# Decay of batch 1 by rank-one matmuls, f by one queue and its chain in two column pieces, under a new instruction order

## The chip, the cores and the metric

The kernel runs on one core of a Trainium2 chip. The metric is the device time of one execution in microseconds (us); less is better. The core has five engines, each with its own instruction queue worked in order: PE (TensorE, matmuls), DVE (VectorE), ACT (ScalarE), POOL (GpSimd) and SP (SyncE, which here only issues DMAs). Engines wait for each other by semaphores alone. Matmuls write to PSUM; ACT and DVE read it.

## The reference

Attention with a forget gate, then a bilinear feed-forward layer. Batch 8, 8 heads, 576 positions, head size 64; 4608 tokens, model width 512, inner width 1536.

```python
def _attn_ref(q, k, v, f):
    scores = scale * np.matmul(q, k.transpose(0, 1, 3, 2))
    log_f = np.log(np.clip(f, 0.0001, 1.0))
    cum = np.cumsum(log_f, axis=-1)
    decay = cum[:, :, :, None] - cum[:, :, None, :]
    scores = np.where(causal, -1000000000.0, scores + decay)
    scores = scores - np.max(scores, axis=-1, keepdims=True)
    attn = np.exp(scores)
    attn = attn / (np.sum(attn, axis=-1, keepdims=True) + 1e-09)
    return np.matmul(attn, v)

def _moe_ref(x, w_a, w_b, w_out):
    a = x @ w_a
    b = x @ w_b
    return a * b @ w_out
```

In a softmax row the term cum of the query is a constant and falls out, so the kernel only adds −cum of the key, a row of 576 numbers for each of 64 heads.

## The kernel before

**Tiling.** Two heads of a batch make a head pair t (t = 4·batch + pair, 0 to 31). The 576 queries of a pair are five row blocks i = 0 to 4 (four of 128, the last of 64), and block i sees i+1 key blocks. Scores are made in four groups: group 0 holds rows 1 and 0, group 1 row 2, group 2 row 3, group 3 row 4. In batches 0 and 1 they come in three PE stages, (0), (1) and (2, 3); later in two. Each group takes one of two PSUM score slots (`sc`). Per row block then follow: the decay and the row maximum on DVE, the exponential with its sum on ACT (L531, L527), the reciprocal on DVE (L541), the normalization on POOL (L549), the transpose of P (batch 0 by PE and an eviction copy, the rest by a DMA transpose that SP issues, L563), P·V on PE (L591, L607) and its copy to xT. The feed-forward layer works on tiles of 256, 384 or 512 tokens: 12 pairs of matmul groups psa and psb (L861), ACT's copy of psa (L213), DVE's product (L872), and the output matmuls pso (L881).

**The decay row.** `f_rows` (L168 to L173) loads f into `cum_f`, 64 heads with two copies each on 128 partitions: one copy by two DMAs of ACT's queue, the other by two of POOL's. Then come, over all 576 columns: clip (DVE, L184), LN (ACT, L186), a running sum with the sign turned (DVE scan, L187), a 16-bit copy (L189) and the low part (L190), which leave `crow`: the sums as a 16-bit high and a 16-bit low row. `cum_store` (L195) also writes the sums to DRAM (`cum_d`).

**Three ways to add the decay.** Batch 0 (`DECP`) adds it on PE: `qk_group` multiplies a column of ones at the head's two rows (`pick`) with `crow` into the score slot, and DVE only takes a maximum over both heads (`do_max`, L474), with ACT's exponential reading PSUM. Batch 1 (`PSPREAD`, t = 4 to 7) has the row spread over 128 partitions by two matmuls a pair (`spread_mm`, L442), copied to the SBUF tile `spread` by ACT or DVE (`spread_ev`), its last 64 columns filled with zeros by POOL (L449; those come from PE in group 3); DVE then adds it head by head in one instruction that also takes the maximum (`do_decay`, L500) and writes a copy of the scores to SBUF tile `S`, from which ACT reads. Batches 2 to 7 load `spread` from `cum_d` (L453), mask it on POOL (L459, L466) and use `do_decay` too.

**Order.** Every step is an `Op` with an engine, a cost for a planner, and what it depends on. The order of all 2336 ops is written out as the list `ORDER`, by op number; `CHOICE` gives the engine of each op that has a choice (P, D, A). Each engine's queue is the part of that list which falls to it. Around the places that matter below, the queues read so. PE at the start: transposes of q and k, scores 0.(0), spread 4, keys' second half, scores 0.(1), spread 4, and so on, with the first feed-forward matmul after pair 0's P transposes. SP, late in batch 1: transpose of pair 6 (rows 2, then rows 3 and 4), load of batch 3's q, transposes of pair 7 (rows 0 and 1; rows 3 and 4), load of batch 3's k, spread of pair 10, transpose of pair 7 (row 2). PE there: four output matmul groups, scores 9.(0), P·V of pair 7's rows 0 and 1, two output groups. The store of the sums is SP's ninth op, behind the first key load of batch 1. POOL's queue begins with its two f loads and the constants, then the casts of q and k.

Of the kernel before, what the change touches and what calls it, by code (L numbers as in the profile page):

```python
# [25 lines left out]
def kernel(  # L26
# [150 lines left out]

    o_f = Op("ACT", 2.05, f_load, prio=-310, land=0.3)
# [5 lines left out]
    o1 = Op("DVE", 0.45, lambda _: nc.vector.tensor_scalar(out=cw["f"], in0=cw["f"], scalar1=1e-4,  # L184
                                                           scalar2=1.0, op0=MAX, op1=MIN), [o_f, o_f2], prio=-300)
    o2 = Op("ACT", 0.7, lambda _: nc.scalar.activation(out=cw["l"], in_=cw["f"], func=LN), [o1, o_w], prio=-300)  # L186
    o3 = Op("DVE", 1.35, lambda _: nc.vector.tensor_tensor_scan(  # L187
        out=cw["f"], data0=cw["1"], data1=cw["l"], initial=0.0, op0=MUL, op1=SUB), [o2, o0], prio=-300)
    o4 = Op("DVE", 0.45, lambda _: nc.vector.tensor_copy(out=cw["h"], in_=cw["f"]), [o3], prio=-300)  # L189
    o5 = Op("DVE", 0.75, lambda _: nc.vector.scalar_tensor_tensor(  # L190
        out=crow, in0=cw["h"], scalar=lowrow[:, 0:1], in1=cw["f"], op0=MUL, op1=ADD), [o4, o_c], prio=-300)
# [4 lines left out]

    o6 = Op("SP", 1.1, cum_store, [o3], prio=-300, land=0.4)
    o_e = Op("ACT", 1.4, warm_table(EXP), [o2], prio=-300)
    for u in s_users:
        u.extend([o_f2, o0, o1, o2, o3, o4, o5, o6])  # L200
# [79 lines left out]
    PSPREAD = {t for t in range(4, 8)}  # L280
    DECP = tuple(range(1))
# [356 lines left out]
    def attention(t, base):  # L638
# [12 lines left out]
        if not direct:  # L651
            if t in PSPREAD:
# [3 lines left out]
                for h in range(2):  # L656
                    bm = Op("PE", 512 * COLS, lambda _, h=h: spread_mm(t, h), [o5, bc0] + bcs, prio=prio(0) - 5, mode="full", name=f"bm{t}")
# [15 lines left out]
        for gs in ([(0,), (1,), (2, 3)] if b in EARLY else [(0, 1), (2, 3)]):  # L673
            deps = [kq_ops[(w, b, pr)] for w in "qk"] + [o_c] + ([o5] if direct else bcs)
# [285 lines left out]
    for n in cuts:  # L960
# [3 lines left out]
        0 1 3 4 19 13 25 31 2 37 20 5 21 6 14 22 7 23 15 26 12 16 260 8 24 11 17 9 54 32 27 18 261 57 28 63 33  # L964
        30 58 262 65 29 59 64 55 263 34 69-71 36 99 264 60 66 35 102 38 39 41 234 10 144 103 108 110 109 104 40
# [3 lines left out]
        56 175 138 220 75 139 81 221 176 183 184 207 87 76-78 241 228 82 229 88 83 242 101 243 118 163 80 79 164  # L969
# [8 lines left out]
        384 385 460 470 301 467 468 289 386 290 296 297 469 291 292 232 1676-1678 479 317 298 1679 374 410 411  # L978
# [4 lines left out]
        1702 1704 420 1703 432 433 428 427 429 1705-1707 421 1708 306 307 1709 399 417 439 440 435 434 1710-1713  # L983
        446 447 441 482 1714 1716 358 1718 1715 442 1719 1720 422 1717 443 489 448 1722-1724 1721 491 498 359
        492 1725 499 505 506 1726 1728 1730 356 1727 493 500 449 357 1729 501 502 436 394 395 400 424 444 431
        430 527 423 445 450 494 490 512 1731 507 508 1732 513 483 488 1733 517 509 484 402 403 655 451 453
        1734-1736 518 495 514 519 520 1739 529 454 1740 531 455 521 532 545 538 539 546 510 438 437 511 497
        503 504 496 522 523 533 1737 1741 1744 1746 408 650 566 452 530 1742 534 1745 540 541 1747 515 516 409
        406 1748 542 535 552 553 547 548 1749-1754 1756 1757 554 537 656 528 536 549 550 544 407 524 1755 557
        1758 1759 485 567 651 551 543 1760-1762 558 555 1763-1765 559 560 1766 1767 657 525 569 1743 608 662 676  # L990
        667 658 1768 659 1769 570 573 1770 1771 456 580 561 457 587 574 581 588 571 652 1772 458 562 556 563-565
        1738 575 653 654 1774 1776 1773 582 576 1777 583 459 1775 1778 572 1780 1779 590 1781 1782 584 577 594
        1783 1784 1786 589 1785 1788-1790 595 1787 596 663 579 568 591 1791 599 600 609 593 585 586 592 668 578
        602 1792-1794 664 1795 601 666 611 615 603 597 598 665 629 616 613 623 617 605 604 660 718 1796 661 677
        719 618 1797-1799 630 622 1800 612 619 1802 625 1803 632 624 631 606 607 674 672 1804 1805 614 636 637
        633 1806 1808 1807 1809 1810 638 1811 610 641 1812 626 1813-1815 642 635 621 634 628 675 620 627 643
# [4 lines left out]
        740 726 1850-1852 741 735 734 728 1853 742 724 746 747 846 760 856 850 761 720 751 752 847 802 848 748  # L1001
        1855-1857 851 717 716 1801 763 753 852 754 861 1854 854 743 729 749 736 1858 730 738 744 737 731 750 767
# [58 lines left out]
        2315 2314 2317 2316 2319 2318 2321 2320 2322 2323 2326 2324 2327 2325 2328 2331 2329 2332-2334 2330 2335  # L1061
# [49 lines left out]
```

## Time and profile before

| what | us |
|---|---|
| median of 3 runs | 418.45 (417.01 to 418.51) |
| the profiled execution | 415.86 |
| its span, first to last instruction | 414.1 |
| DVE decay with maximum, 128-row forms, L500 | 0.28 (128 columns), 0.42 (256), 0.55 (384), 0.68 (512) |
| the same, 64 rows by 576 | 0.75 |
| DVE maximum of both heads, L474 | 0.42, 0.69, 0.96, 1.21; last row 0.75 |
| spread copy from PSUM, 128x512 | 0.68 on DVE, 0.58 on ACT |
| DMA transposes, issue to landing | 3.6 to 8.6, median 4.3 |
| mean granted PE clock | 0.996 of full speed |

A view by stretch gives each engine's busy time between two moments of the span. The timeline lists instructions with start, duration, engine, line and form, and in brackets how long the engine had been idle and what ended that. "SPq" is a DMA issue in SP's queue. The chain of waits follows the last instruction back to what released it, again and again. Durations of matmuls include their latency; the distance from one to the next is their cost in a full PE.

### The profile page before, as it was taken

The page shows a single profiled execution, that of the slowest core. Times are in us where ns is not written, and L with a number is a line of the kernel's source. Part 1 is how long each engine was busy: PE and PEld are TensorE (multiplying, and loading weights), DVE is VectorE, ACT ScalarE, POOL GpSimd, SP SyncE. Part 2 cuts the span into 40 slices and gives each one's busy share as a digit, 9 for nine tenths or more (in the row PEclk, how much of TensorE's full clock was granted, in tenths as well). Part 3 has the DMA queues.
Part 4 walks back from the last instruction along what each step waited for, and adds up shares of the span by engine and source line. Part 5 has one row for each costly group of instructions (what it writes and reads, how often), then busy time and mean ns, then how long its engine had stood idle before and what let it go on. Part 6 is the DMA issues. An engine that isn't in the chain of part 4 may idle for free.

```text
span 414.1 us, 10945 instructions
## 1 busy us (share of the span) xinstructions
PE 391.0 (94%) x3860; PEld 212.0 (51%) x3860; DVE 301.3 (73%) x1002; ACT 276.9 (67%) x788; POOL 254.7 (62%) x442
## 2 busy tenths in 40 slices
PE   0688999998999999999999999999999999999996
PEld 0445785765755544444444544454444444444552
DVE  2889998996878958867987889678777885342240
ACT  2786899775867797766777687687787583231231
POOL 8699698766876867674886687676675745000000
PEclk9999999998999999999999999999999999999999
DMA  8899799999999999999979999999689727300202
GB/s 272 175 220 258 172 210 228 236 206 268 294 239 218 286 229 192 267 215 281 192 206 249 237 271 220 246 211 244 170 181 221 185 57 145 116 1 2 101 2 77
DMA packets 153528, 80.72 MB, mean 195 GB/s; under 512 B 130784, under 2 KB 133344, under 8 KB 153472
## 3 DMA queue, kind: packets, MB, share of 16 engines
q1 hardware_dynamic: 149536, 75.01, 77.1%
q0 software_dynamic: 3856, 4.87, 7.0%
q8 instruction: 30, 0.49, 0.5%
q14 instruction: 26, 0.21, 0.2%
q10 hardware_dynamic: 80, 0.15, 0.1%
HBM read 52.20 MB, written 9.58 MB: 149 GB/s over the span
## 4 chain that ended last, share of the span: by engine, by line
PE 82%; ACT 5%; DVE 4%; DMA 4%; POOL 2%; issue 1%; SPq 1%; POOLq 0%; DVEq 0%; ACTq 0%
PE psa L861 22%; PE pso L881 21%; PE psb L861 21%; PE sc L390 9%; PE pv L591 5%; ACT PA L531 2%; PE psT L258 2%; DMA wout<-in_k_dram 2%; DVE st L474 1%; DMA xT<-PA 1%; PE psP L569 1%; DVE S L500 1%; ACT PB L531 1%; PE sc L607 1%; SPq L563 1%
## 5 line engine op out<-in xcount | busy, mean ns | idle before, releaser
L500 DVE CUSTOM_DVE_ANT_0 S<-sc,spread 64x576 f32<-64x576 f32 (+4 forms) x232 | 125.3, 561 | 8.3 <-PE sc L390 3.5
L861 PE MATMUL psa<-xT,wa 128*128 128x512 f16 (+2 forms) x528 | 115.8, 342 | 0.9 <-DVE ht L872 0.5
L861 PE MATMUL psb<-xT,wb 128*128 128x512 f16 (+2 forms) x528 | 115.6, 342 | 0.3 <-ACT PTB L213 0.3
L549 POOL TENSOR_SCALAR PA<-PA,st 128x128 f16<-128x128 f16 (+2 forms) x192 | 90.1, 483 | 21.0 <-DVE st L541 13.9
L872 DVE TENSOR_TENSOR ht<-psb,a 128x512 f16<-128x512 f32 (+2 forms) x132 | 77.7, 590 | 34.8 <-PE psb L861 28.3
L213 ACT CAST a<-psa 128x512 f16<-128x512 f32 (+2 forms) x132 | 66.4, 504 | 53.4 <-PE psa L861 46.6
L881 PE MATMUL pso<-wout,ht 128*128 128x512 f16 x432 | 99.0, 382 | 0.4 <-DVE osb L217 0.4
L531 ACT ACTIVATE PA<-S,st 128x256 f16<-128x256 f32 (+2 forms) x168 | 84.2, 505 | 12.6 <-DVE st L500 12.5
L549 POOL TENSOR_SCALAR PB<-PB,st 128x512 f16<-128x512 f16 (+1 forms) x96 | 67.8, 715 | 28.1 <-DVE st L541 12.0
L861 PEld LDWEIGHTS <-wb 128*128 128x128 f16 x528 | 50.8, 98 | 40.8 <-issue 0.4
L861 PEld LDWEIGHTS <-wa 128*128 128x128 f16 x528 | 49.0, 98 | 41.3 <-issue 2.6
L881 PEld LDWEIGHTS <-ht 128*128 128x128 f16 x432 | 40.9, 98 | 47.7 <-issue 1.1
L531 ACT ACTIVATE PB<-S,st 128x512 f16<-128x512 f32 x56 | 40.2, 719 | 13.6 <-DVE st L500 12.4
L390 PE MATMUL sc<-kT,qT 64*128 64x128 f16 (+5 forms) x480 | 43.8, 278 | 3.9 <-ACT PA L531 2.2
L531 ACT ACTIVATION_READ_ACCUMULATOR PA<-S,st 128x1 f32 x168 | 32.3, 192 | 0.0
L390 PEld LDWEIGHTS <-qT 64*128 64x128 f16 (+1 forms) x480 | 17.3, 97 | 26.7 <-issue 20.8
L527 ACT ACTIVATE PB<-S,st 128x576 f16<-128x576 f32 x28 | 21.7, 776 | 12.3 <-issue 5.4
L541 DVE RECIPROCAL st<-st 128x2 f32<-128x2 f32 x128 | 18.7, 157 | 14.6 <-ACT PB L531 8.2
L217 DVE CAST xT<-pv 128x512 f16<-128x512 f32 (+1 forms) x40 | 23.0, 576 | 7.5 <-PE pv L591 7.4
L500 DVE CUSTOM_DVE_ANT_1 S<-sc,spread 128x256 f32<-128x256 f32 x48 | 19.8, 419 | 10.3 <-PE sc L607 8.2
L466 POOL TENSOR_SCALAR_AFFINE_SELECT spread<-spread 128x256 f32<-128x256 f32 x24 | 9.8, 408 | 28.0 <-DVE st L500 27.9
L459 POOL TENSOR_SCALAR_AFFINE_SELECT spread<-spread 128x768 f32<-128x768 f32 x24 | 20.9, 872 | 9.1 <-DMA spread<-cum_d 9.1
(85 smaller groups left out, 418.1 us busy)
## 6 DMA issues: line engine op xcount, KB each, us to landing
spread<-cum_d SPq DMA_DIRECT2D x24, 576.0 KB, 5.8
out_dram<-osb SPq DMA_DIRECT2D x36, 256.0 KB, 3.3
q<-in_q_dram SPq DMA_DIRECT2D x15, 576.0 KB, 5.9
k<-in_k_dram SPq DMA_DIRECT2D x15, 576.0 KB, 5.4
v<-in_v_dram SPq DMA_DIRECT2D x32, 256.0 KB, 4.5
wout<-in_moe_w_out_dram POOLq DMA_DIRECT2D x3, 512.0 KB, 6.6
v<-in_v_dram SPq DMA_DIRECT2D x8, 128.0 KB, 5.1
wa<-in_moe_w_a_dram POOLq DMA_DIRECT2D x2, 512.0 KB, 7.5
```

Source lines behind the costliest of these rows:

```text
L213: nc.scalar.copy(out=out_, in_=in_)
L217: VEC[e].tensor_copy(out=out_, in_=in_)
L390: nc.tensor.matmul(out=dst, lhsT=lhsT, rhs=rhs, start=start, stop=stop, skip_group_check=True)
L459: nc.gpsimd.affine_select(out=c[:, :, 0:SM].rearrange("p h (j k) -> p h j k", k=128), in_=c[:, :, SM:2 * SM].rearrange("p h (j k) -> p h j ...
L500: nc.vector.tensor_tensor_reduce(out=o, in0=x, in1=y, scale=-1.0, scalar=3e38, op0=ADD, op1=MIN, accum_out=m)
L527: nc.scalar.activation(out=p_blocks(t, 4), in_=T[("s" if direct else "z", t, 4)], func=EXP, bias=st[:, 8:9], scale=sign, accum_out=st[:, 1 ...
L531: nc.scalar.activation(out=p_blocks(t, i)[:, :, h, :], in_=(T[("s", t, i)][:, h, :] if direct else T[("z", t, i)][:, h * n:h * n + n]).rea ...
L549: VEC[e].tensor_scalar(out=p, in0=p, scalar1=st[:, c:c + 1], scalar2=1.0, op0=MUL, op1=MUL)
L591: nc.tensor.matmul(out=o[HP[h], 128 * i:128 * i + 128], lhsT=vt[:, j, pr + NP * h, :], rhs=pt[:, base_blk[i] + 2 * block_at(t, i, j) + h, ...
L861: nc.tensor.matmul(out=p[:, 0:n], lhsT=w16[:, db, 128 * fb:128 * fb + 128], rhs=xTflat[db][:, t0:t0 + n], start=(db == 0), stop=(db == 3))
L872: nc.vector.tensor_tensor(out=ht[:, 0:n], in0=T.pop(("psb", t0, fb))[:, 0:n], in1=T.pop(("a16", t0, fb))[:, 0:n], op=MUL)
L881: nc.tensor.matmul(out=o, lhsT=T[("ht", t0, fb)][:, 128 * tb:128 * tb + 128], rhs=wout16[:, fb, :], start=(fb == 0), stop=(fb == 11))
```

## The change

`DECP` becomes batches 0 and 1, `PSPREAD` is empty: pairs 4 to 7 get the ones-times-crow matmuls of batch 0, DVE's maximum in place of the decay instruction, and exponentials that read PSUM. Their spread matmuls, spread copies and POOL fills are gone; `spread` and `S` are first used by batch 2. All four f loads are issued by ACT, one after the other. Clip, LN, scan, 16-bit copy and low part run for columns 0 to 255 and then 256 to 575; the second scan starts from the last sum of the first. Score group 0 waits for the first piece alone, the others for both; the table load for EXP waits for both LNs.

There are 2300 ops now, in a newly found order, with 91 engine choices for 99. Near the start: both q casts of the first half on DVE, ahead of the clip; two weight loads on POOL ahead of a q cast; scores 1.(0) ahead of the second half of q; four of the P-transpose copies moved from ACT to DVE and four key and query copies the other way; one value cast moved from DVE to POOL. On SP the store of the sums stands behind the first q load of batch 2, and late in batch 1 the queue reads: spread 10, load of batch 3's k, transposes of pair 6 (rows 3 and 4) and pair 7 (rows 0 and 1), load of batch 3's q, transposes of pair 6 (row 2), pair 7 (rows 3 and 4; row 2). PE's order around pair 7's P·V is the same as before, and the tiles of the feed-forward layer too.

```diff
     def f_load(_):
-        f_rows(nc.scalar, 0)
-
-    def f_rows(eng, c):
-        if not cw:
-            f_tiles()
         rows = f.rearrange("b (h p) s -> h b p s", h=2)
         for half in range(2):
-            eng.dma_start(out=cw["f"][64 * half + 32 * c:64 * half + 32 * c + 32, :], in_=rows[half])
+            for c in range(2):
+                nc.scalar.dma_start(out=cw["f"][64 * half + 32 * c:64 * half + 32 * c + 32, :], in_=rows[half])
...
+    def scan(lo, hi):
+        nc.vector.tensor_tensor_scan(out=cw["f"][:, lo:hi], data0=cw["1"][:, lo:hi], data1=cw["l"][:, lo:hi],
+                                     initial=cw["f"][:, lo - 1:lo] if lo else 0.0, op0=MUL, op1=SUB)
...
-    o_f2 = Op("POOL", 1.3, lambda _: f_rows(nc.gpsimd, 1), prio=-310, land=0.3)
...
+    for lo, hi in ((0, 256), (256, S)):
+        n = hi - lo
+        o1 = Op("DVE", 0.06 + 0.00073 * n, lambda _, lo=lo, hi=hi: clip(lo, hi), [o_f], prio=-300, name="fclip")
+        o2 = Op("ACT", 0.2 + 0.00083 * n, lambda _, lo=lo, hi=hi: nc.scalar.activation(
+            out=cw["l"][:, lo:hi], in_=cw["f"][:, lo:hi], func=LN), [o1, o_w], prio=-300, name="fln")
+        o3 = Op("DVE", 0.02 + 0.00232 * n, lambda _, lo=lo, hi=hi: scan(lo, hi), [o2, o0] + ([o3] if lo else []),
+                prio=-300, name="fscan")
...
-    PSPREAD = {t for t in range(4, 8)}
-    DECP = tuple(range(1))
+    PSPREAD = set()
+    DECP = tuple(range(2))
...
-            deps = [kq_ops[(w, b, pr)] for w in "qk"] + [o_c] + ([o5] if direct else bcs)
+            deps = [kq_ops[(w, b, pr)] for w in "qk"] + [o_c] + (crow_ops[:1 if gs == (0,) else 2] if direct else bcs)
...
     CHOICE = """
-        DPAAPPADPPADAPDAPDPAAAADDDDADDADDDDDDDDAADAADDDDDAAAAAADAADAAAADAADAAAAAADAAADAAAAADDADAADAAAAAAAAA
+        DPAADDAAPPADAPDAPPPDDDDDADDDDDDDAADAADAADAADADAADAADAADAADAADDAAAAAAAAAAADAAAAAAAADADAAADAA
```

More of the change, by code (lines that the diff above doesn't have):

```diff
@@ L165, in f_load, with clip, low_part, cum_store @@
     def f_load(_):
-        f_rows(nc.scalar, 0)
-    def f_rows(eng, c):
-        if not cw:
-            f_tiles()
         rows = f.rearrange("b (h p) s -> h b p s", h=2)
         for half in range(2):
-            eng.dma_start(out=cw["f"][64 * half + 32 * c:64 * half + 32 * c + 32, :], in_=rows[half])
+            for c in range(2):
+                nc.scalar.dma_start(out=cw["f"][64 * half + 32 * c:64 * half + 32 * c + 32, :], in_=rows[half])
     def warm_table(func):
         return lambda _: nc.scalar.activation(out=warm, in_=warm, func=func)
-    o_f = Op("ACT", 2.05, f_load, prio=-310, land=0.3)
+    def clip(lo, hi):
+        x = cw["f"][:, lo:hi]
+        nc.vector.tensor_scalar(out=x, in0=x, scalar1=1e-4, scalar2=1.0, op0=MAX, op1=MIN)
+    def scan(lo, hi):
+        nc.vector.tensor_tensor_scan(out=cw["f"][:, lo:hi], data0=cw["1"][:, lo:hi], data1=cw["l"][:, lo:hi],
+                                     initial=cw["f"][:, lo - 1:lo] if lo else 0.0, op0=MUL, op1=SUB)
+    def low_part(lo, hi):
+        nc.vector.scalar_tensor_tensor(out=crow[:, lo:hi], in0=cw["h"][:, lo:hi], scalar=lowrow[:, 0:1],
+                                       in1=cw["f"][:, lo:hi], op0=MUL, op1=ADD)
+    def cum_store(_):
+        for half in range(2):
+            nc.sync.dma_start(out=cum_d[:, half * S:half * S + S], in_=cw["f"][64 * half:64 * half + 32, :])
+    f_tiles()
+    o_f = Op("ACT", 4.05, f_load, prio=-310, land=0.3)
     s_users = [take(o_f, "S") for _ in range(2)]
-    o_f2 = Op("POOL", 1.3, lambda _: f_rows(nc.gpsimd, 1), prio=-310, land=0.3)
     o_c = Op("POOL", 4.5, lambda _: constants(), prio=-300)
@@ L183 @@
     o_w = Op("ACT", 2.2, warm_table(LN), [o0], prio=-300)
[L184 to L191, printed above, removed]
-    def cum_store(_):
-        for half in range(2):
-            nc.sync.dma_start(out=cum_d[:, half * S:half * S + S], in_=cw["f"][64 * half:64 * half + 32, :])
+    crow_ops, lns = [], []
+    o3 = None
+    for lo, hi in ((0, 256), (256, S)):
[5 more added lines that the diff above has]
+                prio=-300, name="fscan")
+        o4 = Op("DVE", 0.06 + 0.0007 * n, lambda _, lo=lo, hi=hi: nc.vector.tensor_copy(
+            out=cw["h"][:, lo:hi], in_=cw["f"][:, lo:hi]), [o3], prio=-300, name="fhi")
+        o5 = Op("DVE", 0.06 + 0.0013 * n, lambda _, lo=lo, hi=hi: low_part(lo, hi), [o4, o_c], prio=-300, name="flo")
+        crow_ops.append(o5)
+        lns.append(o2)
+        for u in s_users:
+            u.extend([o0, o1, o2, o3, o4, o5])
     o6 = Op("SP", 1.1, cum_store, [o3], prio=-300, land=0.4)
-    o_e = Op("ACT", 1.4, warm_table(EXP), [o2], prio=-300)
+    o_e = Op("ACT", 1.4, warm_table(EXP), lns, prio=-300)
     for u in s_users:
-        u.extend([o_f2, o0, o1, o2, o3, o4, o5, o6])
+        u.append(o6)
     o_p = Op("POOL", 4.0, lambda _: paddings(), [o_c], prio=-100)
@@ L656, in attention @@
                 for h in range(2):
-                    bm = Op("PE", 512 * COLS, lambda _, h=h: spread_mm(t, h), [o5, bc0] + bcs, prio=prio(0) - 5, mode="full", name=f"bm{t}")
+                    bm = Op("PE", 512 * COLS, lambda _, h=h: spread_mm(t, h), crow_ops + [bc0] + bcs, prio=prio(0) - 5, mode="full", name=f"bm{t}")
                     su = take(bm, "ff")
@@ L984 @@
[L984 to L993, printed above, removed]
@@ new lines @@
+        602 1775 625 585 574 597 599 639 592 605 1778 1780 1779 1777 606 633 643 607 635 634 1781 647 648 655
+        654 608 609 603 1782 1784 1783 1785 644 649 1786 1788 1790 661 662 645 1787 657 650 651 656 663 1789
+        1791-1793 646 1794 598 584 610 591 604 653 1765 682 636 808 724 612 611 668 809 1796 664 1795 1797 1798
+        613 1760 813 669 642 683 637 1799-1802 1804 1803 670 658 673 665 666 1805 674 667 659 1806 1808 1807 675
+        1810 676 1811 1812 671 1809 677 1813 679 652 660 672 678 685 810 1814 1815 689 703 697 687 690 696 704
@@ new lines @@
+        691 1816 692 698 706 1817 699 811 812 688 814 815 686 710 711 705 816 712 820 821 684 725 680 681 766
+        700 715 717 716 718 817 1819-1821 1824 727 1825 1826 713 719 693 731 745 707 714 721 701 708 720 746
+        1822 738 733 747 748 729 732 739 694 695 709 702 1818 818 825 1829 1831 740 1827 1830 741 734 1833 1834
+        1832 728 730 723 722 749 752 822 1835 753 826 726 767 1836 823 1837 824 754 1839 757 758 1838 759 755
+        1840-1842 760 769 761 771 773 787 780 742 781 788 774 819 750 762 763 743 756 751 744 827 1843 1844
@@ new lines @@
+        828 829 775 1845 1847 783 782 776 1846 772 1849 1850 790 789 1851 770 784 777 735-737 794 1848 795 1852
+        768 791 834 1823 832 1828 786 833 779 835 793 876 765 764 830 1853 1855 1854 799 800 1856-1858 796 797
+        801 802 778 792 785 1859 837 1861 1863 841 843 848 1862 850 918 1860 855 803 804 842 1864 839 856 838
+        849 1865 1867 1866 1868 798 805 857 858 851 852 1869 1870 844 859 919 853 877 840 862 845 860 854
+        1871-1875 847 846 863 864 1876 836 861 1002 1003 831 867 1877-1879 865 868-870 1880 806 1007 807 874 879
@@ new lines @@
+        1397 1312 1334 1335 1310 1398 2053 1399 1329 2054 1330 2055-2057 1408 1308 1417 2059 2058 1339 1331 1317
+        1319 1333 1324 1326 1340 2060 1318 1336 1341-1343 1325 1332 2061 2062 1304 1305 2063 1351 2064 1355
+        1362 1363 2065 2067 1400 2069 1344 1345 1357 2066 1365 1352 1353 1337 1369 1338 1356 1358 2068 1370 1359
+        2071 2070 1372 2072-2074 1364 1371 2075 2076 1354 1409-1411 2077 1376 1377 1373 1366 1403 1350 1381 2079
+        1378 2078 1383 1379 1382 1375 1374 1384 2080 1414 1346 1347 2032 1458 2027 2081 2082 1419 2083 2086 1423
@@ new lines @@
+        1530 1536 2134 1535 2135 1549 1511 2136 1531 1550 1553 1560 1561 1537 1567 1525 1554 1551 1568 2137 2139
+        2138 1555 2140 2141 1562 1569 1556 2142 1563 2143 1552 2145 1557 2144 1574 1564 1532 1513 1527 2146 1570
+        2147 1575 2148 1576 2149-2151 1538 1520 1526 1512 1539 1559 1540 1541 2154 2155 1558 1548 1565 1566 1579
+        1577 1580 1571 1573 1578 1572 1581 2152 1582 1583 2156 2159 2160 2157 1585 1584 2161 1542 2164 1543
+        1586 1587 2153 2158 2162 2165 1588 2166 1589 2167 2168 2163 2169-2171 2173 2175 2172 2174 2176 2177 2179
@@ L1062 @@
+        2293 2296-2298 2294 2299
     """
     CHOICE = """
-        DPAAPPADPPADAPDAPDPAAAADDDDADDADDDDDDDDAADAADDDDDAAAAAADAADAAAADAADAAAAAADAAADAAAAADDADAADAAAAAAAAA
+        DPAADDAAPPADAPDAPPPDDDDDADDDDDDDAADAADAADADAADADAADAADAADAADDAAAAAAAAAAADAAAAAAAADADAAAADAA
     """
```

85 lines of the change are left out of this document (30 added, 55 removed), and 75 rows, old and new, of the table ORDER.

## The prediction

> **What bounds the kernel now.** I read the page's busy shares first, then the busy time by stretch of the span, then the timeline at the two places where TensorE stands still, then the chain of waits.
>
> ```profile
> span 414.1 us, 10945 instructions
> PE 391.0 (94%) x3860; PEld 212.0 (51%) x3860; DVE 301.3 (73%) x1002; ACT 276.9 (67%) x788; POOL 254.7 (62%) x442
> ```
>
> TensorE (PE) is the bound on average, with 23 us idle. The stretches (us of the span, the stretch's length, then each engine's busy time, clock, DMA share, GB/s) say where:
>
> ```profile
> 0.00:10.00 10.00, 0.84 (x18) 0.53 (x18) 1.79 (x4) 1.91 (x3) 8.12 (x35) 1.00 0.81 272
> 10.00:14.82 4.82, 2.12 (x35) 1.50 (x35) 3.98 (x5) 3.86 (x7) 4.68 (x9) 1.00 1.27 220
> 14.82:38.70 23.88, 20.24 (x262) 12.34 (x262) 21.12 (x47) 17.84 (x61) 19.41 (x38) 1.00 0.99 220
> 38.70:90.00 51.30, 50.38 (x733) 36.10 (x731) 48.14 (x176) 45.62 (x140) 40.99 (x64) 1.00 1.05 211
> 90.00:100.00 10.00, 8.15 (x47) 3.79 (x45) 6.11 (x26) 4.96 (x16) 6.58 (x12) 0.83 1.08 249
> 100.00:400.00 300.00, 299.04 (x2723) 152.99 (x2723) 217.79 (x743) 200.56 (x562) 174.91 (x289) 1.00 0.82 192
> ```
>
> Until 14.8 the inputs and the decay row are the bound; from there to 38.7 (first feed-forward matmul) VectorE (DVE, 21.1 of 23.9 us) and batch 0's softmax; from 38.7 on PE, full but for one hole in 90 to 100, where the clock falls as well. After 100 the hole is under 1 us in 300, so whatever is gained or lost before 100 reaches the end unshortened. The two places (start, duration, engine):
>
> ```profile
> 8.81 0.73 DVE L184 TENSOR_SCALAR cum_f<-cum_f 128x576 f32<-128x576 f32 x1 [7.24 <-DMA cum_f<-in_f_dram]
> 12.73 1.28 DVE L190 SCALAR_TENSOR_TENSOR crow<-cum_l,lowrow,cum_f 128x576 f16<-128x576 f16 x1
> 14.07 0.50 PE L390 MATMUL sc<-crow,pick 64*128 64x256 f16 x4 [0.68 <-DVE crow L190]
> 14.82 1.02 DVE L474 TENSOR_REDUCE st<-sc 128x2 f32<-128x512 f32 x2 [0.81 <-PE sc L390]
> ...
> 89.60 0.98 SPq L243 DMA_DIRECT2D q<-in_q_dram  x1
> ...
> 90.69 1.23 SPq L563 DMA_TRANSPOSE xT<-PA  x1
> ...
> 95.44 0.36 PE L591 MATMUL pv<-xT,nv 128*64 128x128 f16 x6 [1.85 <-DMA xT<-PA]
> ```
>
> The clip of f waits for f's load until 8.81; crow is ready at 14.01 and the first scores end with it, although the keys were there at 12.88. At the second place head pair 7's P·V waits for a transpose that was queued behind a q load.
>
> **The change, term by term.**
>
> *Head.* The four f loads go out on ACT's queue. The two there now took 2.02 us, so four take about 4.0 and end near 4.85; the last begins near 3.85, against 2.2 for POOL's last now. The f loads and the stores of the sums took 3.6 to 6.3 us to land, so f lands at 7.5 to 10.2; I take 8.8, as now, near the middle. ACT's table load moves from 2.87 to about 4.9 and ends near 6.2: hidden. POOL loses 1.35 us of issue, so the constants end at about 5.8 for 7.2. The q casts move to VectorE, which waited until 8.81 anyway, at some 0.8 us each (its k cast took 0.83), after q has landed (4.0 us after 0.81): done by 6.5, with k by 7.4, so keys and queries are ready before f. From f's landing: clip of 256 columns 0.33 (0.73·256/576), LN 0.30 (of 0.68), scan 0.60 (of 1.36), cast 0.20, low part 0.57, and 0.1 for each of four handovers: 2.4 us, crow's first piece at 11.2. The second piece needs scan 0.76, cast 0.26, low part 0.71: 12.95. VectorE then takes its first maximum at 13.0, which now starts at 14.82: **−1.8**. ACT is ready for it: key copies at 10 to 11.3, the EXP table (1.28 and 0.20), a q cast 0.63 and a key copy 0.65 end near 14.0, and the first exponential now starts at 15.94. Ends: f at 7.5 gives −3.1, f at 10.2 gives −0.4; a further us of slip in the casts, +0.6.
>
> [...]
>
> *14.8 to 38.7.* Six of the eight spread matmuls go (cold, 0.54 us from one to the next, 3.2 us), with five VectorE copies of 0.68 (3.4 us of 21.1) and ACT's one of 0.58. In the chain of waits these hold ACT 0.47, PE 0.54 and 0.54, VectorE 0.60 and 0.60: 2.75 us. The new order also hands copies between ACT and VectorE: four P-transpose copies (2.7 us) go to VectorE, four key and query copies (3.0) leave it, so that evens out, and the second value cast (0.69) goes to POOL, which loses three fills of 0.2. Ends 0 (other work fills the places) and −2.75; I take **−1.5**, since VectorE was 88% busy and most of its loss counts.
>
> *PE in batch 1, 46 to 86.* Each head pair gains ten crow matmuls, 64-row halves side by side. In the chain of waits the two-group stage costs 1.24 us with the decay (18 matmuls) and 0.81 without (14): +0.43. The first two groups have 384 columns each; 256 columns take 0.11 at full clock (four feed-forward matmuls of 256 in 0.44), so 0.16 each. 0.75 a pair, 3.0 for four; the last pair's two warm spread matmuls (0.32 and 0.22) go: **+2.5**. PE is full there, so all of it counts; ends +1.9 (some of it falls into the 0.9 us of holes) and +3.0.
>
> *VectorE and ACT in batch 1.* Per pair ten decays (2·(281+417+548+681)+2·753 ns = 5.36 us) become five maxima (417+690+958+1213+746 ns = 4.02): 5.3 us less over four, off the bound. It costs nothing and brings nothing by itself; it helps the next term. The exponentials read PSUM for SBUF at the same length (476 against 508 ns for 256). What is lost is the early release of the score slots, the first rival.
>
> *The hole at 93.6 to 95.4.* PE idles 1.85 us and then runs at half clock: eight output matmuls 2.64 for 1.80, two feed-forward groups 0.85 each for 0.44, so 0.84+0.41+0.41 = 1.66 more; 3.5 together. In the new SP order pair 7's first transpose stands ahead of that q load (0.98 us and gaps, 1.1), PE reaches the place 2.5 us later against the softmax, and VectorE there is lighter. Both together are more than 1.85. Ends −3.5 (gone, with the clock loss) and +2 (the hole doubles, since a later transpose, pair 6's second, now stands behind the q load). I take **−2.5**, near the end where it closes.
>
> [...]
>
> *Costed at nothing.* The store of the sums moves in SP's queue from behind the first key load of batch 1 to behind a q load of batch 2 (issued at 46.2 now), with only the spread of pair 8 waiting for it, wanted after 80: 30 us of cover; without it the 3.7 us store and a 5.8 us spread load are bare. Weight loads move ahead on POOL, to about 10 us for 19.06: two issues of 0.67 in front of a q cast; they crowd the value loads, which nothing reads before the first P·V at 30.2. The rest of the order after 100 has the same matmuls; ends −0.9 (its hole) and +3.5 (one new hole like that at 94).
>
> Sum: −1.8 −1.5 +2.5 −2.5 = −3.3. The profiled execution took 415.86 (span 414.1 and 1.8 around it) and would be 412.6; it lies 2.6 under the median 418.45 of the runs shown, so I forecast 418.45 − 3.3 = **415.1**.
>
> **Rivals.** *Score slots hold PE, slower.* A score slot of batch 1 is now freed by VectorE's last decay; then by ACT's last exponential: for the first group a maximum pair (1.1) and four exponentials (1.8), 2.9 us for 1.1. With two slots, PE's next scores wait, and all feed-forward matmuls behind them in order. Batch 0 has just this: PE waited 2.2 us for ACT's PA exponentials and 0.2 for its PB. Against it: some 11 us pass per pair in batch 1 and the slots need about (2.9+2.2+2.6+1.5)/2 = 4.6. Price: 2.4 again in a full PE, one clock loss of 1.7, the hole left as it is: −1.8 −0.8 +2.5 +2.4 +1.7 = +4.0, **422.4**. It decides once such waits exceed about 3 us. *The hole stays.* Transposes take 3.6 to 8.6 us to land whatever stands ahead: −0.8, **417.6**. *f late by one queue.* f at 10.2: −3.3+1.4 = −1.9, **416.5**. *The order is no better on the chip than on paper* (a new hole after 100, +3.5): 0.2, 418.6.
>
> **How the numbers follow.** Half a per cent is 2.1 us, about what this kernel's runs can tell from no change. Forecast 0.48, slots 0.26, hole stays 0.10, f late 0.08, new hole 0.08. Faster takes the forecast, less 0.04 where its terms come out small, and half of f late: 0.48. Slower takes the slots and half of the new hole: 0.30. Same: 0.22. The likeliest case alone lies in 412 to 417; for 8 in 10 I go down to 411 (head and stretch at their ends, −7) and up to 422 (the slots' case, whose upper half is left out).
>
> **What would show it.** Clip near 8.8 and the first maximum near 13.0; first feed-forward matmul near 35.4 instead of 38.7; no idle over 1 us and no clock under 1.00 in 85 to 100; PE waits on ACT's exponentials in batch 1 under 1 us in sum. It is wrong if PE sits idle before score matmuls between 45 and 90, if f lands past 10, or if a stretch after 100 shows a clock under 1.00.

## The result and the profile after

The changed kernel takes 423.89 us (median of 4 runs, 421.49 to 425.69), the kernel before 417.73 beside it (4 runs, 416.90 to 418.51): a ratio of 1.0137, with a 95% interval of 1.0103 to 1.0171. It is 1.4% slower, where 0.8% faster was forecast, and it lies above the range. The profiled execution took 425.69 with a span of 424.0. So the two profiles stand 9.8 us apart while the medians differ by 6.2: before's profile (415.86) lies 1.9 below its median, the one after 1.8 above. Differences between the two profiles are read with that in mind.

The page after, span and busy time, and the same stretches as before (length, busy time with instructions of PE, weight load, DVE, ACT and POOL, clock, DMA share, GB/s):

```profile
span 424.0 us, 10909 instructions
...
PE 392.0 (92%) x3892; PEld 214.2 (51%) x3892; DVE 295.6 (70%) x943; ACT 273.8 (65%) x785; POOL 251.3 (59%) x435
```

```profile
0.00:10.00 10.00, 1.69 (x36) 1.10 (x37) 2.01 (x5) 2.67 (x4) 5.48 (x30) 1.00 0.83 265
10.00:14.82 4.82, 2.00 (x40) 1.66 (x41) 3.73 (x7) 3.59 (x7) 4.28 (x9) 1.00 1.25 194
14.82:38.70 23.88, 14.93 (x217) 10.39 (x214) 18.09 (x41) 16.67 (x60) 18.59 (x34) 0.93 0.82 186
38.70:90.00 51.30, 48.61 (x724) 34.27 (x717) 41.09 (x99) 38.22 (x119) 37.45 (x57) 1.00 0.99 209
90.00:100.00 10.00, 9.79 (x94) 5.95 (x91) 7.77 (x31) 5.53 (x21) 7.01 (x14) 1.00 1.09 229
100.00:400.00 300.00, 294.73 (x2683) 150.03 (x2683) 216.53 (x752) 201.18 (x566) 178.52 (x297) 0.99 0.86 196
```

DVE is 7 us lighter from 38.7 to 90, as the change meant, and 90 to 100 is fuller. But PE, which was full from 38.7 on, now loses 2.7 us there, 5.3 in the 300 us after 100 (before: 1.0), and from 14.8 to 38.7 it is 5.3 us less busy (45 matmuls fewer, at a clock of 0.93). In that last stretch DVE, ACT and POOL are less busy as well.

The place at the start, and that of a new hole at 190, in the timeline (start, duration, engine, line, form; in brackets the idle time before and what ended it):

```profile
0.80 3.44 ACTq L169 DMA_DIRECT2D cum_f<-in_f_dram  x4
...
10.65 0.75 DVE L176 TENSOR_SCALAR cum_f<-cum_f 128x256 f32<-128x256 f32 x2 [3.69 <-DMA v<-in_v_dram]
11.20 0.78 ACT L201 ACTIVATE cum_l<-cum_f 128x256 f32<-128x256 f32 x2 [3.82 <-DVE cum_f L176]
...
11.88 1.16 ACT L228 COPY kT<-psT 128x576 f16<-128x576 f16 x2
...
12.55 0.50 PE L405 MATMUL sc<-kT,qT 64*128 64x256 f16 x4 [4.52 <-ACT kT L228]
...
13.19 1.33 DVE L179 TENSOR_TENSOR_SCAN cum_f<-cum_f,cum_l 128x320 f32<-128x320 f16 x1
...
15.31 1.23 DVE L183 SCALAR_TENSOR_TENSOR crow<-cum_l,lowrow,cum_f 128x320 f16<-128x320 f16 x1
...
16.46 1.94 DVE L489 TENSOR_REDUCE st<-sc 128x2 f32<-128x512 f32 x4
...
179.41 3.71 SPq L578 DMA_TRANSPOSE PTA<-PA  x1
183.16 0.58 SPq L258 DMA_DIRECT2D q<-in_q_dram  x1
183.84 3.41 SPq L578 DMA_TRANSPOSE PTB<-PB  x1
...
192.29 0.25 PE L606 MATMUL pv<-PTB,nv 128*64 128x128 f16 x2 [1.62 <-DMA PTB<-PB]
```

The clip starts at 10.65 (before 8.81). The releaser in its bracket is a v load that landed about then; what it needs is f. ACT's key copies stand behind both LNs in ACT's queue, so PE has no scores until 12.55. The second piece then holds DVE until 16.5, and only behind it comes the first maximum, at 16.46 (before 14.82), although its scores were complete at 14.05.

PE's waits (us in total, times, longest):

```profile
PE sc L405 <- ACT PA L546: 6.7, 5, 3.0
PE psT L273 <- DVE q L230: 5.2, 1, 5.2
PE sc L405 <- ACT kT L228: 4.5, 1, 4.5
PE pv L606 <- DMA PTB<-PB: 2.6, 3, 1.6
```

The first row is the wait for a score slot; it was 2.2 us before. All but 0.3 us of it falls into batch 0, ahead of the first feed-forward matmul. At 190.7 PE stands 1.62 us for the transpose that was issued at 183.84 and landed at 192.24, and then runs at half clock for 3.4 us. It also ran at half clock for 3.4 us at 32.1. The mean granted clock was 0.992 in two of the four runs (spans 423.8 and 424.0, the second being the profiled one) and 0.999 and 1.000 in the others (419.8 and 420.6); where the other run with 0.992 lost it is not on record.

**One common measure.** The table lists moments of the span at which a feed-forward matmul (psa, psb or pso) of a given number starts, and PE's idle time (gaps over 0.2 us, added up from each kernel's matmul records) in the parts between them. The labels are those of the experiments below.

| kernel | 1st | 193rd | 289th | last | idle: before 1st | to 193rd | to 289th | after | sum |
|---|---|---|---|---|---|---|---|---|---|
| before | 38.7 | 85.4 | 107.7 | 409.9 | 14.8 | 0.6 | 1.8 | 0.8 | 18.0 |
| after | 39.0 | 91.7 | 111.2 | 419.9 | 19.7 | 2.4 | 2.1 | 2.8 | 27.0 |
| b_1q | 40.7 | 87.3 | 108.7 | 413.5 | 17.9 | 0.6 | 2.4 | 2.9 | 23.8 |
| b_dec | 37.9 | 96.5 | 115.0 | 422.4 | 17.6 | 6.2 | 0 | 5.3 | 29.1 |
| a_2q1p | 36.2 | 89.3 | 110.5 | 417.5 | 18.1 | 2.8 | 2.4 | 3.3 | 26.6 |
| a_2q | 35.4 | 87.9 | 108.1 | 414.1 | 17.0 | 2.7 | 2.6 | 2.3 | 24.6 |
| a_2q_nocrow | 35.4 | 87.6 | 107.3 | 414.3 | 17.2 | 4.1 | 2.3 | 3.3 | 26.9 |

Each row is one execution. A second profile of a_2q has the same first two moments within 0.1 us, but the 289th 1.1 us and the last 0.9 us earlier; so differences of a microsecond between rows mean little.

The last matmuls of before and after are 10.0 us apart, and PE's idle times 9.0. But 4.9 of this idle time stands ahead of the first feed-forward matmul, which comes only 0.2 us later, as less work stands ahead of it. Behind that matmul lie 9.7 us. By the distances from one matmul to the next they are: PE idle +4.1, crow matmuls +3.0, spread matmuls −0.5, 14 transposes of P that stood ahead of it before +1.6, and about 1.5 in small differences.

### The profile page after: what moved, and what is told of

It is laid out like the page before. It is cut to its first block, busy times and chain, and to the rows that moved or that the text cites. A ratio compares the mean times of both kernels' runs of the same rounds, so it can differ in the third digit from the quotient of the medians.

```text
span 424.0 us, 10909 instructions
## 1 busy us (share of the span) xinstructions
PE 392.0 (92%) x3892; PEld 214.2 (51%) x3892; DVE 295.6 (70%) x943; ACT 273.8 (65%) x785; POOL 251.3 (59%) x435
## 5 line engine op out<-in xcount | busy, mean ns | idle before, releaser
L515 DVE CUSTOM_DVE_ANT_0 S<-sc,spread 64x576 f32<-64x576 f32 (+2 forms) x192 | 105.6, 567 | 7.5 <-POOL spread L481 3.6
L564 POOL TENSOR_SCALAR PA<-PA,st 128x256 f16<-128x256 f16 (+2 forms) x192 | 89.4, 478 | 25.2 <-DVE st L556 21.2
L546 ACT ACTIVATE PA<-S,st 128x256 f16<-128x256 f32 (+2 forms) x144 | 72.1, 503 | 14.4 <-DVE st L515 14.4
L405 PE MATMUL sc<-kT,qT 64*128 64x256 f16 (+5 forms) x480 | 44.7, 279 | 13.0 <-ACT PA L546 6.7
L546 ACT ACTIVATE PB<-S,st 128x512 f16<-128x512 f32 x48 | 34.4, 717 | 10.7 <-DVE st L515 10.4
L489 DVE TENSOR_REDUCE st<-sc 128x2 f32<-128x512 f32 (+4 forms) x40 | 31.4, 802 | 3.4 <-PE sc L405 2.6
L546 ACT ACTIVATION_READ_ACCUMULATOR PA<-S,st 128x1 f32 x144 | 27.4, 190 | 0.0
L232 DVE COPY osb<-pso 128x512 f32<-128x512 f32 x17 | 11.7, 689 | 21.7 <-PE pso L896 21.6
```

Of the source, the lines that this page charges most:

```text
L232: VEC[e].tensor_copy(out=out_, in_=in_)
L405: nc.tensor.matmul(out=dst, lhsT=lhsT, rhs=rhs, start=start, stop=stop, skip_group_check=True)
L489: nc.vector.tensor_reduce(out=m, in_=T[("s", t, i)], axis=AXX, op=MAX, negate=True)
L515: nc.vector.tensor_tensor_reduce(out=o, in0=x, in1=y, scale=-1.0, scalar=3e38, op0=ADD, op1=MIN, accum_out=m)
L546: nc.scalar.activation(out=p_blocks(t, i)[:, :, h, :], in_=(T[("s", t, i)][:, h, :] if direct else T[("z", t, i)][:, h * n:h * n + n]).rea ...
L564: VEC[e].tensor_scalar(out=p, in0=p, scalar1=st[:, c:c + 1], scalar2=1.0, op0=MUL, op1=MUL)
```

## The experiments

Labels with b_ are edits of the kernel before in its own order, with a_ of the changed kernel in the new order. Ratios are against the kernel before, run beside them.

### The change in its parts

**b_dec**: the decay of batch 1 alone, in the old order (without the spread instructions; seven score stages and one maximum stand a few places later, where a score slot is free).

```diff
-    PSPREAD = {t for t in range(4, 8)}
-    DECP = tuple(range(1))
+    PSPREAD = set()
+    DECP = tuple(range(2))
```

> The kernel before with the decay of batch 1 on PE alone: f by two queues, the chain in one piece and the order of before (score stages of pairs 3 to 8 a few places later, so that a score slot is free). Theory 'head, decay and holes each have a share': PE pays 2.5 us after 38.7, VectorE's relief gives 1.5 back before it, the hole at 94 closes in part: -1 to +2 us against before. Rival 'score slots': PE waits for ACT's exponentials between 45 and 90 for over 2 us, +4 us or more. Rival 'only the order and the f chain cost': the forecast holds without them, -2 us or better.

429.10 us, ratio 1.0275 (1.0232 to 1.0318). Its waits of PE, and what stands at the longest one:

```profile
PE sc L390 <- ACT PA L531: 9.1, 9, 2.7
```

```profile
45.92 1.61 DVE L474 TENSOR_REDUCE st<-sc 128x2 f32<-128x512 f32 x2
...
47.52 0.40 DVE L474 TENSOR_REDUCE st<-sc 128x2 f32<-128x256 f32 x1
...
47.96 0.47 ACT L531 ACTIVATE PA<-sc,st 128x256 f16<-128x256 f32 x1 [0.60 <-DVE st L474]
```

Scores made at 45.3 are read by the maximum, and only then by ACT's exponentials from 47.96; PE stands 2.68 us at 48.0 for that slot and then runs at half clock for 6.8 us. The first rival's mechanism is real. In the old order PE's waits for these slots grow from 2.2 to 9.1 us over the whole span, where the prediction had 2.4 more; b_dec as a whole costs 11.6 us. The spread's own relief is small: the first feed-forward matmul comes 0.8 us earlier.

**b_f**: the new f part alone (one queue, two pieces) in the old order. It is every part of the change's diff but those of `PSPREAD`, `DECP` and the new order.

> The kernel before with the new f chain alone: four f loads on ACT's queue, the chain in two column pieces, in the order of before; decay of batch 1 by spreads. Theory: f lands near 10.6 instead of 8.8 and VectorE's first maximum begins 2 to 3 us later (near 17.3 for 14.8); the delay reaches the first feed-forward matmul in part: +1 to +2.5 us. Rival 'the head is hidden behind batch 0's softmax': below +0.5 us.

420.99 us, 1.0088 (1.0054 to 1.0122). The clip:

```profile
10.56 1.30 DVE L176 TENSOR_SCALAR cum_f<-cum_f 128x256 f32<-128x256 f32 x2 [8.99 <-DMA cum_f<-in_f_dram]
```

f is late in this order as well; the piece of the change that was to gain 1.8 us costs 0.9%.

**a_2q1p**: the changed kernel with f by two queues and its chain in one piece, as before.

```diff
+    o_f2 = Op("POOL", 1.3, lambda _: f_rows(nc.gpsimd, 1), prio=-310, land=0.3, name="f_load2")
-    for lo, hi in ((0, 256), (256, S)):
+    for lo, hi in ((0, S),):
```

> The changed kernel with f by two queues and the chain in one piece, as before; decay on PE and the new order kept. Theory: f lands near 8.8, the first maximum begins near 13.6 instead of 16.5, and 1.5 to 3 us come back: 421 to 422.5 for 423.9. Rival 'the order alone costs': less than 0.5 us comes back.

423.84 us, 1.0137 (1.0103 to 1.0171): no gain over the changed kernel, as its rival said, although the first maximum came at 14.90 and the first feed-forward matmul at 36.2, 2.8 us earlier than after. By the 289th only 0.7 of that is left. PE stood 2.39 us at 97.4 here and ran at half clock for 3.4 us. In the medians nothing of the gain at the head reaches the end.

**a_2q**: f by two queues, with the two pieces kept. **a_2q_again** is the same kernel, timed over ten executions.

> The changed kernel with f by two queues, the chain still in two pieces. Theory: f lands near 8.8, the clip begins 1.8 us earlier than in the changed kernel, and the first maximum near 14.7 for 16.5; the chain in one piece brought it near 13.6, so the pieces themselves cost 1 us. Rival 'the pieces are free': the first maximum at 13.6 or earlier.

> The changed kernel with f by two queues and two pieces, timed in rounds. Theory: first feed-forward matmul 3.5 us earlier than in the changed kernel, 2.5 to 3.5 us of it at the end, 420.5 to 421.5. Rival 'lost again on the way': 423 to 424.

420.43, then 420.20 us, 1.0060 (1.0033 to 1.0088). Here f lands when it was forecast to:

```profile
8.56 0.53 DVE L178 TENSOR_SCALAR cum_f<-cum_f 128x256 f32<-128x256 f32 x2 [1.17 <-DMA cum_f<-in_f_dram]
...
11.15 0.48 DVE L185 SCALAR_TENSOR_TENSOR crow<-cum_l,lowrow,cum_f 128x256 f16<-128x256 f16 x1
...
14.10 1.02 DVE L492 TENSOR_REDUCE st<-sc 128x2 f32<-128x512 f32 x2
```

The first maximum comes at 14.10, 1.1 us behind the forecast's 13.0, and the first feed-forward matmul at 35.4, which is the forecast's 35.4: the stretch between them is 21.3 us and not 22.4, so two errors cancel, and that is luck. Against the changed kernel 0.0077 of the ratio comes back, some 3.2 us of 417.7, and the intervals do not meet. One queue for f is thus about half of the 6.2 us lost. The rest is in this kernel still: on time until 35.4, and slower than before.

**b_1q** and **b_2p**: one queue alone, and two pieces alone, in the old order.

```diff
-        f_rows(nc.scalar, 0)
+        for half in range(2):
+            for c in range(2):
+                nc.scalar.dma_start(out=cw["f"][64 * half + 32 * c:64 * half + 32 * c + 32, :], in_=rows[half])
```

> The kernel before with all four f loads on ACT's queue, the chain in one piece, everything else as before. Theory: the clip begins near 10.6 for 8.8 and 1.5 to 2.5 us of it reach the end; the rest of the 3.5 us of the f chain alone is the pieces'. Rival 'the pieces cost it all': below 0.5 us.

> The kernel before with f by two queues and the chain in two pieces, in the order of before (both pieces end before the first maximum). Theory: the two pieces make VectorE's chain some 1 us longer there, +0.5 to +1.5 us. Rival 'the pieces are free or a gain': 0 or less.

421.06 us, 1.0082 (1.0053 to 1.0111), and 419.52 us, 1.0035 (1.0012 to 1.0058). One queue gives b_f's loss by itself. In all profiles of this case with f by one queue (six) the clip starts at 10.45 to 11.35, in all with two (fourteen) at 8.47 to 9.33. Two pieces do not pay in the old order: its first maximum came at 15.93 for 14.82. In the new order they do (a_2q against a_2q1p), so the two parts hang on each other and on the order.

**a_spread**: the new order with batch 1's decay by spread, as before; the diff of b_dec turned around, with the spread's instructions put in where the old order has them.

> The changed kernel with batch 1's decay by spreads as before, in the new order (spread matmuls and copies put behind the same neighbours as in the old order, the store of the sums behind the first key load of batch 1, spread loads of pairs 8 and 9 later); f by one queue in two pieces. Theory 'the decay on PE costs in the new order too': 1.5 to 4 us less than the changed kernel, 420 to 422.5. Rival 'the new order is what costs': 424 or more.

432.70 us, 1.0345 (1.0295 to 1.0395).

```profile
PE pv L622 <- DMA PTB<-PB: 5.8, 2, 4.1
```

The last row block's P·V at 78 stands 4.1 us for its transpose. In these placings decay on PE and the new order need each other: either alone costs 2.8 and 3.5 per cent (with f by two queues in b_dec, by one here), both together 1.4, and 0.6 with f by two queues. Each of the two kernels has instructions put into an order that was found without them, at one set of places only; how much of its price is the placing was not tried.

### Is PE the bound in batch 1?

**a_nocrow** (changed kernel), **a_2q_nocrow** (a_2q) and **b_dec_nocrow** (b_dec) make everything but the ones-times-crow matmuls of batch 1, so its decay is left out. These are 48: the 40 that the change adds, and 8 for the last 64 columns that the kernel before has too.

```diff
-            if b in DECP:
+            if b == 0:
                 for h, r in enumerate(HP):
                     mm(c[r, 0, :], ones[h], crow[r, 0:512], stop=True)
```

> The changed kernel without the ones-times-crow matmuls of batch 1 (40 of them; the decay of batch 1 is left out), the order as it is. Theory 'PE is the bound after 38.7': 3.0 us less by the 130th feed-forward matmul, and as much at the end, 421 for 423.9. Rival 'what is won before 100 is lost again to transposes that land no earlier': 3 us less at 77, below 1 us at the end.

> The changed kernel with f by two queues and without the ones-times-crow matmuls of batch 1 (the decay of batch 1 is left out). Theory 'the queue of f and the decay's matmuls are two shares that add': 1.0137 less 0.0077 less 0.0065, so 0.997 to 1.002 of before. Rival 'each covers the other': 1.005 or more.

> The kernel before with batch 1's maxima and exponentials on the score slots as in the change, in the old order, but without the ones-times-crow matmuls of batch 1 (its decay is left out). Theory 'the score slots hold PE in the old order': most of the 11.6 us stays, 425 or more, with PE waiting over 1.5 us at 48 for ACT's exponentials. Rival 'the matmuls are the price': 420 or less.

| kernel | us | ratio to before | its parent's ratio |
|---|---|---|---|
| a_nocrow | 421.47 | 1.0072 (1.0040 to 1.0104) | 1.0137 (1.0103 to 1.0171) |
| a_2q_nocrow | 420.21 | 1.0066 (1.0039 to 1.0093) | 1.0060 (1.0033 to 1.0088) |
| b_dec_nocrow | 424.37 | 1.0161 (1.0121 to 1.0201) | 1.0275 (1.0232 to 1.0318) |

The second row decides. The stretch 38.7 to 90 of a_2q, then of a_2q_nocrow:

```profile
38.70:90.00 51.30, 48.48 (x717) 34.02 (x716) 40.74 (x106) 38.76 (x122) 39.21 (x60) 1.00 1.01 211
```

```profile
38.70:90.00 51.30, 46.59 (x670) 32.35 (x667) 40.67 (x108) 38.85 (x123) 39.34 (x60) 1.00 1.05 219
```

The matmuls are gone: 47 fewer, 1.9 us less busy. DVE, ACT and POOL did the same work within 0.2 us, the 193rd feed-forward matmul came 0.3 us earlier, the 289th 0.8 and the last 0.2 later, all within what two profiles of one kernel differ by, and the time is the same. Over the whole span PE is 2.4 us less busy (386.7 for 389.1) and 2.3 more idle. So with f on time PE's work does not set the pace there, though it is 94% busy. With f late, leaving it out brought 0.65%, its interval just touching the parent's; in b_dec 1.1%, of a loss of 2.75, between what its theory and its rival said.

### The holes

**b_hole**: the kernel before, with the q load that stood ahead of pair 7's first transpose put behind it.

```diff
 SP: ...
-    load of batch 3's q
     transpose of pair 7, rows 0 and 1
+    load of batch 3's q
```

> The kernel before with one DMA issue moved: the q load of batch 3 on SP behind the transpose of pair 7's rows 0 and 1. Theory: the hole at 93.6 goes because that transpose is issued about 1 us earlier; with the clock kept, 1.5 to 3.5 us less than before. Rival 'the hole is set by how late POOL's normalizations and the landing are': below 0.5 us of difference, a hole of over 1 us stays.

418.02 us, 0.9993 (0.9968 to 1.0017). The hole at 93.6 is gone, and:

```profile
97.93 5.24 SPq L563 DMA_TRANSPOSE PTA<-PA  x1
...
106.18 0.41 PE L591 MATMUL pv<-PTA,nv 128*64 128x128 f16 x6 [2.02 <-DMA PTA<-PA]
```

a hole of 2.02 us stands ten microseconds on, and a clock loss with it (half clock for 6.8 us). So the term of −2.5 for closing the hole brings nothing by itself.

**a_tr** and **a_2q_tr**: the changed kernel, and a_2q, with the load of batch 5's q behind the transpose that the hole at 190 waits for.

```diff
 SP: ...
-    load of batch 5's q
     transpose of pair 15, rows 3 and 4
+    load of batch 5's q
```

> The changed kernel with one DMA issue moved: the q load of batch 5 on SP behind the transpose of pair 15's rows 3 and 4. Theory: the hole at 190 (1.62 us idle and then half clock, 3.9 us in all) comes from that transpose landing late; it is issued about 0.7 us earlier, the hole is below 1 us and the clock stays: 420 to 421.5, all runs near the lower pair. Rival 'the hole is a matter of how the DMA engines are loaded, not of this load': spread and median as they were, 422 to 425.

> The changed kernel with both: f by two queues, and the q load of batch 5 behind the transpose of pair 15's rows 3 and 4. Theory 'head and hole are separate shares': 417.5 to 419, within 0.3% of before. Rival 'each gain only uncovers the next hole': 420.5 or more.

421.07 us, 1.0082 (1.0054 to 1.0110), and 420.07 us, 1.0055 (1.0035 to 1.0074). The hole at 190 is gone in both; a_tr has another of 1.30 us at 144.4. In the changed kernel the move is worth about half a per cent, with intervals that still overlap a little; in a_2q, nothing. The two repairs, f (0.77%) and this one (0.55%), do not add up: with both the ratio stays at 1.0055, not near 1.

### What is left, and a way to beat both

**b_dve**: the kernel before with both first q casts on DVE, as in the new order, and nothing else. **a_2q_cs**: a_2q with the store of the sums on SP as early as before. **a_2q_trA**: a_2q with pairs 4 and 6 normalized earlier on POOL and their first transposes earlier on SP. **a_2q_pb3**: a_2q with a third tile for P of rows 3 and 4.

```diff
-    "PB": 2, ... "ht": 14
+    "PB": 3, ... "ht": 12
```

> The kernel before with the two casts of q's first half on VectorE ahead of the clip instead of on POOL, as the new order has it. Theory: PE's first transposes begin near 5.2 instead of 7.9, but the first scores still wait for crow at 14: within 0.3% of before. Rival 'the early start is worth something': 1 us or more less.

> The changed kernel with f by two queues and the store of the sums on SP where it was, behind the first key load of batch 1, instead of behind the q load of batch 2. Theory 'the store was not free: on SP it holds the second q load of batch 2 for 2 us, whose cast stands on POOL ahead of pair 4's last normalization and so of batch 1's transposes': 1 to 2.5 us less than with f by two queues alone (1.0060), 1.000 to 1.004. Rival 'the store is hidden': 1.005 to 1.007.

> The changed kernel with f by two queues and two normalizations of pairs 4 and 6 ahead of batch 2's q casts on POOL, the first transposes of pairs 4 and 6 ahead of and behind the second q load on SP; the store of the sums stays late. Theory 'batch 1's transposes begin late (69 us, 62.7 before) and pace what follows': they begin 5 us or more earlier and 1 to 3 us are won, 1.000 to 1.004. Rival 'the transposes of rows 3 and 4 and the P slots pace it, not these': 1.005 to 1.007.

> The changed kernel with f by two queues and three P tiles for rows 2, 3 and 4's part B (PB) instead of two, paid for with 12 ht tiles instead of 14; same order. Theory 'PB tiles, held until their DMA transpose has landed, pace batch 1 from 60 to 97': ACT's waits for a PB tile go and 1 to 3 us are won, 1.000 to 1.004. Rival: 1.005 to 1.007, or more if the fewer ht tiles hold VectorE.

| kernel | us | ratio to before |
|---|---|---|
| b_dve | 417.63 | 1.0001 (0.9975 to 1.0028) |
| a_2q_cs | 420.53 | 1.0055 (1.0028 to 1.0082) |
| a_2q_trA | 422.42 | 1.0099 (1.0063 to 1.0136) |
| a_2q_pb3 | 422.81 | 1.0094 (1.0063 to 1.0126) |

The casts on DVE bring 0.8 us at the first feed-forward matmul (38.0 for 38.7) and nothing at the end. The late store is hidden, as forecast. The other two do not help: their medians lie 0.3 to 0.4% above a_2q's, though the intervals overlap. Both did what they were to do. In a_2q_trA the first DMA transposes are issued at 59.96 and 62.08, in a_2q at 69.37; in a_2q_pb3 ACT's two waits for a PB tile, in a_2q 1.2 us until 74.7 and 5.3 until 97.8, are gone. Yet from the first to the last feed-forward matmul they take 378.2 and 378.8 us, and a_2q 378.7 and 377.8 in its two profiles. The fewer `ht` tiles of a_2q_pb3 may hide a gain, which was not separated. No kernel tried is faster than the one before.

## Why the prediction was wrong, by its steps

**Head, −1.8: this step failed first, measured +1.6.** It took f's landing as 8.8, "as now, near the middle", between 7.5 and 10.2. In the changed kernel the clip started at 10.65, past the upper end. The four issues on ACT end at 4.24, those of two loads at 2.83 (0.81 and 2.02): 1.4 us later, and the clip is 1.84 later. The bounds came from the landings of POOL's f loads and of the stores of the sums, counted from their issue; the row that decided was the one on record for f itself, that clip starts at 8.81 with half the issues ahead of it. The 1.4 us by which the issues end later are most of the 1.84 that were given away. Then the chain: forecast 4.2 us from clip to maximum, measured 5.8 (5.5 in a_2q), because the second piece did not scale with its columns (scan 1.33 for 0.76, cast 0.71 for 0.26, low part 1.23 for 0.71). That the key copies wait on ACT behind the LNs costs nothing there, as the scores were complete before DVE was free. With f by two queues (a_2q) the step and the next one give 35.4 together, as forecast, but each is off by 1.1 us. In the end f's queue is worth 0.77 to 0.82% (a_2q, b_1q), some 3.3 us, and not the 1.4 of the rival "f late by one queue", which had a chance of 0.08. That rival was about half of what happened.

**14.8 to 38.7, −1.5: right in number, in part by luck.** Maximum to first feed-forward matmul was 23.9 us and is 22.5 (39.0 − 16.46): −1.4. But 14 transposes of P now come after that matmul (the 44 in the stretch took 4.07 us by their distances, the 30 left take 2.62), and their time returns in the next step; the forecast did not have this. In a_2q the stretch is 21.3 us, −2.6. PE waits 6.4 us for score slots there, and the stretch is no longer for it.

**PE in batch 1, +2.5, "PE is full there, so all of it counts": the mechanism failed.** From the 1st to the 193rd feed-forward matmul it is 6.0 us more (52.7 for 46.7). In a_2q, from the 1st to the 289th, 72.7 us for 69.0; and as about 1.5 us of matmuls that stood there come later now, 5.2 more. By the distances from one matmul to the next: crow +3.0, spread −0.5, the 14 transposes +1.5, PE idle +2.9, and the half-clock stretch at the old hole −1.7. So the sum of the matmuls was right, but leaving them out (a_2q_nocrow) does not bring them back. Waits for other engines and DMAs took their place. The prediction put the other engines' costs in batch 1 at nothing because PE was full before; it did not ask whether it would still be full in another order.

**The hole, −2.5: half right for the place, wrong for the time.** The hole moved from 93.6 to 99.9 and is 1.58 us for 1.85, without a clock loss (1.00 in both stretches): about 1.9 us by the numbers of the forecast (0.27 and 1.66). b_hole shows that the place alone is worth nothing at the end.

**"Whatever is gained or lost before 100 reaches the end unshortened": false.** a_2q1p gained 2.8 us at 39 and nothing at the end, b_dve 0.8 at 38 and nothing; in b_hole one hole closed and another opened. Losses were not simply passed on either: b_1q was 1.9 us late at the first feed-forward matmul, 1.0 at the 289th and 3.6 at the last, with 2.1 us more idle behind the 289th.

**Costed at nothing.** The store of the sums: right (a_2q_cs). The order after 100: the upper end, +3.5 for "one new hole like that at 94", is what happened at 190 in the profiled run (1.62 us idle and 3.4 at half clock); two of the four runs kept their clock (0.999 and 1.000).

**The rivals.** Score slots in batch 1: refuted in the new order (PE waited 1.1 us there for ACT's exponentials, near the "under 1 us" that was to show the forecast right), and true in the old one (b_dec). Of the three signs of being wrong two came: f past 10, and a stretch after 100 with a clock under 1.00. What the range missed was that the rivals were taken one at a time. f late, a hole that stays, and a new hole after 100 came together, and no case held more than one of them.

**Open.** What paces PE in the new order with f on time, where 2.3 to 2.8 us (0.55 to 0.66%) remain through a_2q, a_2q_again, a_2q_tr, a_2q_nocrow and a_2q_cs. The chain of waits of a_2q_nocrow from 60 to 97 runs through the transposes of rows 3 and 4 and a k load:

```profile
62.38 6.49 DMA k<-in_k_dram
68.86 5.21 DMA PTB<-PB
...
80.89 3.84 DMA PTB<-PB
...
88.55 8.35 DMA PTB<-PB
```

That SP's transposes pace it is argued from this chain only. Two edits that should have loosened it (transposes 9 us earlier in a_2q_trA, no wait for a PB tile in a_2q_pb3) brought nothing, so it is not shown. The kernel with one queue and one piece in the new order was not tried.

## What to carry to other kernels

Before a busy engine is called the bound of a stage, leave some of its work out: PE, 94% busy, gave back none of 2.4 us here (a_2q_nocrow), because waits took their place, 2.3 us more idle. A small load that everything at the start hangs on should not have its issues in one queue: here the clip behind it started at 10.45 to 11.35 us with one queue and at 8.47 to 9.33 with two, and the price at the end was nearly twice the delay, 3.2 to 3.4 us for 1.84. In an order written out by hand a gain at one place counts only as far as the next wait comes earlier too, and the rivals of a prediction that touches several places have to be added up, not only taken one by one.

## What the runs showed of the hardware beyond that

**Half clock lasted 3.4, 6.8 or 10.2 us.** The granted clock was 0.50 for 3.4 us at 96.7 in the kernel before and at 32.1 and 192.5 in the one after, for 6.8 at 49.7 in b_dec, and for 10.2 and 6.8 at 24.4 and 106.3 in b_hole (a mean clock of 0.98 over its 417.0 us). The length of the idle time ahead does not tell here whether it comes: it came behind 1.85 us idle (before, at 93.6) and 1.62 (after, at 190.7), and not behind 1.58 (after, at 99.9) or 2.16 (a_2q, at 96.2, where the clock was 1.00 from 90 to 110).

**The same DVE instruction varies up to almost threefold at the start.** The scan of 576 columns took 1.36 us before and 1.84 in a_2q1p, the cast of 576 columns 0.46 and 1.27 in the same two, the low part 1.28 and 0.82; the cast of 320 columns in the changed kernel 0.71, more than the 0.46 of 576 before. POOL was busy beside all of them, with other instructions each time; which of these makes the difference was not tried.
